# One rotation of three PSUM banks for the scores and the products with the values

## The chip, the cores and the metric

The kernel runs on one core of a Trainium2 chip. The metric is the device time of one launch in microseconds; lower is better. A time is the median of several runs on the chip; beside it stands one execution recorded by the hardware profiler, whose trace is read here.

## What is computed

Attention over four batches of eight heads (768 positions, head size 64), where a query sees the first four keys (the sinks) and the 128 keys up to its own position, followed by a feed-forward block with a short convolution as its gate. In the reference, cut to what matters:

```python
scores = scale * np.matmul(q, k.transpose(0, 1, 3, 2))
keep = is_sink | in_window            # 4 sinks, window of 128
scores = np.where(keep, scores, -1000000000.0)
a = np.exp(scores - np.max(scores, axis=-1, keepdims=True))
a = a / (np.sum(a, axis=-1, keepdims=True) + 1e-09)
x = np.matmul(a, v)                    # heads side by side: 512 columns
h = np.maximum(x @ w_in, 0.0)          # 512 -> 1024
conv_out = sum(conv_w[k] * shifted(h, k) for k in range(3))
out = (h / (1.0 + np.exp(-conv_out))) @ w_out
```

## The kernel before

The work goes by pairs of heads: 16 pairs g (four to a batch), each with six query tiles t of 128 rows. Three query tiles make a half. The first batch runs half 0 of its four pairs, then half 1 of each; from the second batch on, both halves of a pair follow each other. That gives 96 steps. Three slots of a step i work on three different steps:

- slot 0, `scores(g, t)` (L440): TensorE forms the scores of the two heads into two PSUM tiles `sc` (L319, or L322 and L323 from pair 4 on, where each product is split in two). VectorE patches the window edge (L457) and takes the row minimum of the negated, masked scores while writing them to SBUF as `pe` (L458). ScalarE takes the exponential (L461), VectorE the reciprocal of the sum (L463, L464), and GpSimd multiplies (L466).
- slot 1, `transp`, one step later: TensorE transposes `pe` into the PSUM tile `pts` (L481), ScalarE copies it to SBUF as `pT` (L483), GpSimd cuts the two triangles of the window (L485, L487). After the third tile of a half the sink columns are transposed too (L492 to L495, tile `tk`, result `sT`).
- slot 2, `pv`, two steps later and only after the third tile of a half: TensorE multiplies the values with `pT` (L512) and the sink part with `sT` (L515) into one PSUM tile `px` of 128x384. `xout` evacuates it with a ScalarE cast (L330, `xH`) and a VectorE subtraction (L331, `xL`), which together are the split operand of the feed-forward block.

The feed-forward block (`Moe`) works in units: 12 matmuls `ph` (L174), a chain over ScalarE, VectorE and GpSimd (L181 to L192), and six matmuls `po` (L201). It can start on a batch only when all four pairs of that batch have gone through `xout`. Its matmuls are handed out evenly between the slots while the next batch's attention runs, so TensorE has them to fill with; during the first 12 steps it has none. The feed-forward weights arrive in double width and are narrowed in those first steps (L102 to L105 and L112, L113, 16 tiles and the taps).

PSUM has eight banks here: two for `ph` and the transposes of q, k and sinks, two for `po`, one for `pts`, two for `sc` and one for `px`. A tile with a tag and `bufs=n` takes the next of n buffers in the order of the code, and waits until the last reader of that buffer's previous tile is through. A scheduler then orders the instructions of all engines by its own estimate of when each is ready, within these waits; the lists it makes are fixed when the kernel is built, and each engine works through its list in order. So on TensorE an instruction that waits holds up everything behind it in its list.

Of the kernel before, what the change touches and what calls it, by code (L numbers as in the profile page):

```python
# [10 lines left out]
F32 = mybir.dt.float32  # L11
# [6 lines left out]
P = 128  # L18
# [5 lines left out]
SW = 2 * P + NS  # L24
# [339 lines left out]
def banded(c):  # L364
# [8 lines left out]
    ap, ps = A.ap, A.ps  # L373
# [64 lines left out]
    def scores(g, t):  # L438
        s = st[g]
        lo = 0 if t == 0 else (t - 1) * KW  # L440
        mk = m0 if t == 0 else (m1 if t == 1 else m2)
        cols = slice(NS if t == 0 else 0, KW)
        sm = ap.tile([P, 6], F32, tag="sm", name=f"sm{g}_{t}", bufs=5)
        hf, u = divmod(t, 3)
        if u == 0:
            s.pe[hf] = ap.tile([P, 3, 2, KW], F32, tag="pe", name=f"pe{g}_{hf}")
            if t == 0:
                nc.gpsimd.memset(s.pe[hf][:, 0, :, 0:NS], 0.0)
        pe = s.pe[hf][:, u]
        pcs = [ps.tile([P, SW], F32, tag="sc", name=f"sc{g}_{t}_{j}", bufs=2) for j in range(2)]  # L450
        if t == 0:
            A.scores(s, t, [pc[:, KW:SW] for pc in pcs], lo, lo + P)
        else:
            A.scores(s, t, pcs, lo, lo + SW)
        for j, pc in enumerate(pcs):
            if t:
                nc.vector.copy_predicated(pc[:, KW:SW], before.bitcast(I32), pc[:, 0:P])  # L457
            nc.vector.tensor_tensor_reduce(out=pe[:, j, cols], in0=pc[:, P:SW][:, cols], in1=mk, op0=ALU.add, op1=ALU.min,  # L458
                                           scale=1.0, scalar=3.0e38, accum_out=sm[:, j:j + 1])
        for j in range(2):  # L460
            nc.scalar.activation(pe[:, j, cols], pe[:, j, cols], AF.Exp, bias=sm[:, j:j + 1], scale=-1.0,  # L461
                                 accum_out=sm[:, 2 + j:3 + j])
        nc.vector.tensor_scalar(sm[:, 2:4], sm[:, 2:4], 1e-9, None, ALU.add)  # L463
        nc.vector.reciprocal(sm[:, 4:6], sm[:, 2:4])  # L464
        for j in range(2):
            nc.gpsimd.tensor_scalar(pe[:, j, cols], pe[:, j, cols], sm[:, 4 + j:5 + j], 1.0, ALU.mult, ALU.mult)  # L466
# [30 lines left out]
    def pv(g, t):  # L497

        s = st[g]
        hp = g % NPAIR  # L500
        hf, u = divmod(t, 3)
        if u < 2:
            return
        px = ps.tile([P, 3, P], F32, tag="px", name=f"px{g}_{hf}").rearrange("p t k -> p (t k)")
        first = 3 * hf
        tiles = range(first + 2, max(0, first - 1) - 1, -1)
        for kt in tiles:
            pT = s.pT.pop((kt, hf)).rearrange("p h a k -> p h (a k)")
            lo, hi = max(kt, first), min(kt + 1, first + 2)
            cols = slice(P * (lo - kt), P * (hi - kt) + P)  # L510
            for j in range(2):
                nc.tensor.matmul(px[D * j:D * j + D, P * (lo - first):P * (hi - first) + P], s.v[:, kt, j, :], pT[:, j, cols],  # L512
                                 start=(kt == tiles[0]), stop=False, skip_group_check=True)
        for w in range(1 - hf, 3):
            nc.tensor.matmul(px[:, P * w:P * w + P], c.vs[:, w, P * hp:P * hp + P], s.sT, start=False, stop=(w == 2),  # L515
                             skip_group_check=True)
        A.xout(g, hf, px)
# [51 lines left out]
    for i in range(NST + D2):  # L569
        if i < NST:  # L570
            n, g, t = steps[i]
# [13 lines left out]
        for slot in range(SLOTS):  # L585
            if slot == 0 and i < NST:
                scores(g, t)
            if slot == 1 and 0 <= i - D1 < NST:
                transp(*steps[i - D1][1:])
            if slot == 2 and 0 <= i - D2 < NST:  # L590
                pv(*steps[i - D2][1:])
                if i - D2 + 1 in cuts:
                    while fill:
                        fill.pop(0)()
                    lo, hi, span = cuts[i - D2 + 1]
                    fill = m.pieces(lo, hi)
                    rate = len(fill) / (span - 0.5)
                    acc = 0.0
            acc += rate / SLOTS
            while acc >= 1.0 and fill:  # L600
                fill.pop(0)()
                acc -= 1.0
            while todo and i + (slot + 1) / SLOTS >= todo[0][0]:
                todo.pop(0)[1]()
# [143 lines left out]
```

## Time and profile before

| | |
|---|---|
| runs | 498.47, 500.34, 500.88 us, median 500.34 |
| the profiled execution | 500.05 us; its span in the trace 498.3 us |
| granted TensorE clock, mean of the span | 0.985 |
| HBM read and written | 27.65 MB and 6.29 MB |
| instructions on VectorE / ScalarE / GpSimd | 1176 / 1084 / 620 |

The span runs from the first to the last recorded instruction. "Busy" is the share of the span in which an engine ran something; PEld is TensorE's loading of stationary operands beside its matmuls. The waits view lists, for an engine and a line, which instruction of which engine ended its idle time, with the total in us, the number of waits and the longest. The timeline gives start, duration, engine, line, operation and tiles. The windows view gives busy time of each engine in a stretch, then the granted TensorE clock, the DMA share and GB/s. The product tiles `px` start at 27.29, 37.73, 45.28 and 49.83 us for half 0 of the first four pairs, at 61.72 for half 1 of pair 0, and the last one at 421.05 us.

### The profile page before, as it was taken

The page shows a single profiled execution, that of the slowest core. Times are in us where ns is not written, and L with a number is a line of the kernel's source. Part 1 is how long each engine was busy: PE and PEld are TensorE (multiplying, and loading weights), DVE is VectorE, ACT ScalarE, POOL GpSimd, SP SyncE. Part 2 cuts the span into 40 slices and gives each one's busy share as a digit, 9 for nine tenths or more (in the row PEclk, how much of TensorE's full clock was granted, in tenths as well). Part 3 has the DMA queues.
Part 4 walks back from the last instruction along what each step waited for, and adds up shares of the span by engine and source line. Part 5 has one row for each costly group of instructions (what it writes and reads, how often), then busy time and mean ns, then how long its engine had stood idle before and what let it go on. Part 6 is the DMA issues. An engine that isn't in the chain of part 4 may idle for free.

```text
span 498.3 us, 10547 instructions
## 1 busy us (share of the span) xinstructions
PE 464.8 (93%) x3209; PEld 398.1 (80%) x3209; DVE 351.4 (71%) x1176; ACT 341.7 (69%) x1084; POOL 322.6 (65%) x620
## 2 busy tenths in 40 slices
PE   3868879799999999999999999999999999999994
PEld 2546668588888888888888888888889888899982
DVE  5788989778857786867677777776585674655551
ACT  3979768678777967867777777776776664545542
POOL 2589899966866776685856677575755555344341
PEclk9999979999999999999999999999999999999999
DMA  5958652435234241514142333303011100101001
GB/s 124 261 154 216 204 135 66 101 80 141 60 70 100 74 112 35 140 34 97 37 100 53 70 90 72 99 18 95 24 54 34 42 3 2 42 1 43 8 36 51
DMA packets 85990, 39.59 MB, mean 79 GB/s; under 512 B 79244, under 2 KB 79268, under 8 KB 85924
## 3 DMA queue, kind: packets, MB, share of 16 engines
q1 hardware_dynamic: 85924, 38.82, 29.7%
q8 instruction: 28, 0.46, 0.4%
q14 instruction: 38, 0.31, 0.2%
HBM read 27.65 MB, written 6.29 MB: 68 GB/s over the span
## 4 chain that ended last, share of the span: by engine, by line
PE 81%; DVE 10%; POOL 3%; DMA 2%; ACT 2%; issue 2%; SPq 0%; DVEq 0%; ACTq 0%; POOLq 0%
PE ph L174 27%; PE po L201 26%; PE px L512 8%; PE sc L322 4%; PE pts L481 4%; PE px L515 4%; PE sc L323 3%; PE tq L261 2%; POOL pe L466 2%; PE sc L319 2%; PE tk L274 1%; DVE stm L104 1%; DVE stm L105 1%; DVE t L186 1%; DVE pe L458 1%
## 5 line engine op out<-in xcount | busy, mean ns | idle before, releaser
L201 PE MATMUL po<-woH,g 128*128 128x512 f32 x384 | 141.0, 408 | 5.5 <-POOL g L191 5.0
L466 POOL TENSOR_SCALAR pe<-pe,sm 128x132 f32<-128x132 f32 (+1 forms) x192 | 84.7, 452 | 49.8 <-DVE sm L464 30.7
L174 PE MATMUL ph<-xH,wiH 128*128 128x258 f32 (+1 forms) x384 | 112.2, 292 | 1.4 <-DVE kk L280 1.4
L174 PE MATMUL ph<-xH,wiL 128*128 128x258 f32 (+1 forms) x384 | 110.2, 287 | 0.0
L174 PE MATMUL ph<-xL,wiH 128*128 128x258 f32 (+1 forms) x384 | 110.0, 287 | 0.0
L461 ACT ACTIVATE pe<-pe,sm 128x132 f32<-128x132 f32 (+1 forms) x192 | 77.2, 405 | 21.1 <-DVE sm L458 20.5
L191 POOL TENSOR_SCALAR g<-t 128x256 fp32r<-128x256 f32 x96 | 41.7, 434 | 76.5 <-DVE t L189 55.0
L186 DVE SCALAR_TENSOR_TENSOR t<-hb,cw,t 128x256 f32<-128x256 f32 x96 | 60.4, 629 | 40.4 <-ACT t L185 39.6
L201 PEld LDWEIGHTS po<-woH,g 128*128 128x128 f32 x384 | 68.8, 189 | 16.1 <-POOL g L191 6.5
L174 PEld LDWEIGHTS ph<-xH,wiH 128*128 128x128 f32 x384 | 73.3, 191 | 4.6 <-issue 1.7
L201 PE MATMUL po<-woL,g 128*128 128x512 f32 x192 | 76.7, 399 | 0.0
L192 POOL TENSOR_TENSOR g<-t,g 128x256 fp32r<-128x256 f32 x96 | 73.0, 761 | 5.5
L174 PEld LDWEIGHTS ph<-xH,wiL 128*128 128x128 f32 x384 | 73.4, 191 | 2.3
L174 PEld LDWEIGHTS ph<-xL,wiH 128*128 128x128 f32 x384 | 73.2, 191 | 1.0
L188 ACT ACTIVATE t<-t 128x256 f32<-128x256 f32 x96 | 40.3, 419 | 36.3 <-DVE t L187 36.0
L457 DVE COPY_PREDICATED sc<-before,sc 128x128 f32<-128x128 int32 x160 | 44.7, 290 | 27.4 <-PE sc L323 19.0
L189 DVE SCALAR_TENSOR_TENSOR t<-t,hb 128x256 f32<-128x256 f32 x96 | 48.6, 507 | 19.4 <-ACT t L188 18.7
L458 DVE CUSTOM_DVE_ANT_0 pe<-sc,m 128x132 f32<-128x132 f32 (+1 forms) x192 | 52.5, 288 | 11.7 <-PE sc L323 9.0
L181 ACT ACTIVATE hb<-ph 128x258 f32<-128x258 f32 (+1 forms) x96 | 36.9, 386 | 29.6 <-PE ph L174 28.0
L187 DVE SCALAR_TENSOR_TENSOR t<-hb,cw,t 128x256 f32<-128x256 f32 x96 | 51.7, 538 | 4.7
L185 ACT ACTIVATE t<-hb,cw 128x256 f32<-128x256 f32 x96 | 49.2, 513 | 7.9 <-POOL g L192 4.0
L512 PE MATMUL px<-pT,vraw 128*64 128x256 f32 (+1 forms) x448 | 48.4, 345 | 3.0 <-POOL pT L487 3.0
(113 smaller groups left out, 943.5 us busy)
## 6 DMA issues: line engine op xcount, KB each, us to landing
raw<-in_q_dram SPq DMA_DIRECT2D x64, 96.0 KB
raw<-in_k_dram SPq DMA_DIRECT2D x64, 96.0 KB
out_dram<-stm SPq DMA_DIRECT2D x24, 256.0 KB
kk<-kk SPq DMA_DIRECT2D x24, 198.0 KB
vraw<-in_v_dram SPq DMA_DIRECT2D x24, 192.0 KB
wi_0r<-in_moe_w_in_dram SPq DMA_DIRECT2D x2, 512.0 KB
wi_1r<-in_moe_w_in_dram SPq DMA_DIRECT2D x2, 512.0 KB
wi_2r<-in_moe_w_in_dram SPq DMA_DIRECT2D x2, 512.0 KB
```

The costliest lines, as they stand in the source:

```text
L174: nc.tensor.matmul(u.h[:, 0:W], w[:, cc, ff * P:(ff + 1) * P], x[:, cc, t0:t1], start=(i == 0), stop=(i == len(prods) - 1))
L185: nc.scalar.mul(a, prev, cw[:, 0, ff:ff + 1])
L186: nc.vector.scalar_tensor_tensor(out=e, in0=this, scalar=cw[:, 1, ff:ff + 1], in1=a, op0=ALU.mult, op1=ALU.add)
L187: nc.vector.scalar_tensor_tensor(out=a, in0=nxt, scalar=cw[:, 2, ff:ff + 1], in1=e, op0=ALU.mult, op1=ALU.add)
L189: nc.vector.scalar_tensor_tensor(out=a, in0=e, scalar=1.0, in1=this, op0=ALU.add, op1=ALU.mult)
L192: nc.gpsimd.tensor_tensor(out=u.g[:, 1], in0=a, in1=f(u.g[:, 0]), op=ALU.subtract)
L201: nc.tensor.matmul(po[:, 0:c.DM], u.g[:, a, tt * P:(tt + 1) * P], w[:, ff, :], start=(ff == 0 and i == 0), stop=(ff == NFF - 1 and i == 2))
L457: nc.vector.copy_predicated(pc[:, KW:SW], before.bitcast(I32), pc[:, 0:P])
L458: nc.vector.tensor_tensor_reduce(out=pe[:, j, cols], in0=pc[:, P:SW][:, cols], in1=mk, op0=ALU.add, op1=ALU.min, scale=1.0, scalar=3.0e38, ...
L461: nc.scalar.activation(pe[:, j, cols], pe[:, j, cols], AF.Exp, bias=sm[:, j:j + 1], scale=-1.0, accum_out=sm[:, 2 + j:3 + j])
L466: nc.gpsimd.tensor_scalar(pe[:, j, cols], pe[:, j, cols], sm[:, 4 + j:5 + j], 1.0, ALU.mult, ALU.mult)
L512: nc.tensor.matmul(px[D * j:D * j + D, P * (lo - first):P * (hi - first) + P], s.v[:, kt, j, :], pT[:, j, cols], start=(kt == tiles[0]), s ...
```

## The change

The tile `px` takes the tag of the score tiles, and that tag gets three buffers in place of two. The number of banks in use stays at eight.

```diff
-        pcs = [ps.tile([P, SW], F32, tag="sc", name=f"sc{g}_{t}_{j}", bufs=2) for j in range(2)]
+        pcs = [ps.tile([P, SW], F32, tag="sc", name=f"sc{g}_{t}_{j}", bufs=3) for j in range(2)]
...
-        px = ps.tile([P, 3, P], F32, tag="px", name=f"px{g}_{hf}").rearrange("p t k -> p (t k)")
+        px = ps.tile([P, 3, P], F32, tag="sc", name=f"px{g}_{hf}", bufs=3).rearrange("p t k -> p (t k)")
```

Six score tiles and one `px` now follow each other through the same three banks, in the order of the code: `px` of a half comes behind the scores of the step two later than the half's last, and ahead of the next step's scores. Every engine's list changes with it, since the scheduler places instructions anew. Three places on TensorE follow. In the names, `sc1_2_0` is the score tile of pair 1, query tile 2, head 0; `px0_0` is the product tile of pair 0, half 0; `pe4_0` holds the weights of attention of pair 4, half 0; the last number of a name only tells instances apart.

The first is TensorE's list in the first stage, around the first product tile (difference of the two lists, - before, + changed):

```order
 L481 MATMUL pts_162<-ident_85,pe1_0_289 128x128 x2
-L319 MATMUL sc2_2_1_514<-kk2_277,X20_319 128x260
 L512 MATMUL px0_0_351<-pT0_2_0_305,vraw0_71 64x128 x2
 L512 MATMUL px0_0_351<-pT0_1_0_273,vraw0_71 64x256 x2
 L512 MATMUL px0_0_351<-pT0_0_0_234,vraw0_71 64x256 x2
 L515 MATMUL px0_0_351<-sT0_0_313,vs_156 128x128 x2
-L319 MATMUL sc3_0_0_546<-kk2_277,X30_447 128x128
+L319 MATMUL sc1_2_0_385<-kk0_163,X10_214 128x260
+L319 MATMUL sc1_2_1_386<-kk0_163,X10_214 128x260
```

Before, 18 score tiles stood ahead of `px0_0` (up to pair 2, tile 2); now 10 do, and the scores of pair 1, tile 2 come directly behind it.

The second is TensorE's list at the end of the product tile of pair 11, half 0. Before:

```order
L322 MATMUL sc12_0_1_4490<-kk4_1164,X120_4259 128x128
L323 MATMUL sc12_0_1_4490<-kk4_1164,X120_4259 128x128
L201 MATMUL po400_4233<-woH_111,g43_4277 128x512
L201 MATMUL po400_4233<-woL_112,g43_4277 128x512
L201 MATMUL po401_4237<-woH_111,g43_4277 128x512
L201 MATMUL po401_4237<-woL_112,g43_4277 128x512
L261 MATMUL tq1210_4376<-identr_90,nq121_4372 128x128 x3
L515 MATMUL px11_0_4397<-sT11_0_4323,vs_156 128x128 x2
```

And in the changed kernel:

```order
L174 MATMUL ph44_4325<-xL1_119,wiH_109 128x258
L481 MATMUL pts_162<-ident_85,pe11_1_4285 128x128
L261 MATMUL tq1210_4376<-identr_90,nq121_4372 128x128 x3
L481 MATMUL pts_162<-ident_85,pe11_1_4285 128x128
L515 MATMUL px11_0_4397<-sT11_0_4323,vs_156 128x128 x2
L322 MATMUL sc12_0_0_4489<-kk4_1164,X120_4259 128x128
L323 MATMUL sc12_0_0_4489<-kk4_1164,X120_4259 128x128
```

Between `px11_0` and `sc12_0_0` the code makes two score tiles (`sc11_5_0` and `sc11_5_1`), so `sc12_0_0` takes the bank of `px11_0`; it stood ahead of the last two matmuls of `px11_0` before and stands directly behind them now. The same neighbours stand at `px10_0` (two transposes between) and at `px14_0` (four matmuls of L201 between).

The third is TensorE's list between the scores of pair 4, tile 0 and their transposes. Before, the last rows ahead of the transposes (the scores `sc4_0_1` stand 28 rows ahead of these transposes, with 12 matmuls of L174 and 6 of L201 ahead of the first row shown):

```order
L481 MATMUL pts_162<-ident_85,pe3_1_1201 128x128 x2
L322 MATMUL sc4_1_0_1449<-kk4_1164,X40_1253 128x260
L323 MATMUL sc4_1_0_1449<-kk4_1164,X40_1253 128x260
L322 MATMUL sc4_1_1_1450<-kk4_1164,X40_1253 128x260
L323 MATMUL sc4_1_1_1450<-kk4_1164,X40_1253 128x260
L493 MATMUL tk3_5_1410<-ident_85,sk3_1_1411 96x128
L201 MATMUL po00_952<-woH_111,g6_1324 128x512
L201 MATMUL po01_992<-woH_111,g6_1324 128x512
L274 MATMUL tk50_1434<-ident_85,raw0_67 128x128 x3
L481 MATMUL pts_162<-ident_85,pe4_0_1384 128x128 x2
```

And in the changed kernel, from the scores themselves:

```order
L322 MATMUL sc4_0_1_1387<-kk4_1164,X40_1253 128x128
L323 MATMUL sc4_0_1_1387<-kk4_1164,X40_1253 128x128
L322 MATMUL sc4_1_0_1449<-kk4_1164,X40_1253 128x260
L323 MATMUL sc4_1_0_1449<-kk4_1164,X40_1253 128x260
L322 MATMUL sc4_1_1_1450<-kk4_1164,X40_1253 128x260
L323 MATMUL sc4_1_1_1450<-kk4_1164,X40_1253 128x260
L201 MATMUL po00_952<-woH_111,g6_1324 128x512
L201 MATMUL po01_992<-woH_111,g6_1324 128x512
L481 MATMUL pts_162<-ident_85,pe3_1_1201 128x128 x2
L493 MATMUL tk3_5_1410<-ident_85,sk3_1_1411 96x128
L274 MATMUL tk50_1434<-ident_85,raw0_67 128x128 x3
L481 MATMUL pts_162<-ident_85,pe4_0_1384 128x128 x2
```

The scores of tile 0 have moved towards their transposes: 12 matmuls of L174 and six of L201 no longer stand between them.

## The prediction, made before the changed kernel ran

> **What bounds the kernel now.** I read the page's totals first, then the stretches, then the waits of TensorE.
>
> ```profile
> span 498.3 us, 10547 instructions
> PE 464.8 (93%) x3209; PEld 398.1 (80%) x3209; DVE 351.4 (71%) x1176; ACT 341.7 (69%) x1084; POOL 322.6 (65%) x620
> PE 81%; DVE 10%; POOL 3%; DMA 2%; ACT 2%; issue 2%; SPq 0%; DVEq 0%; ACTq 0%; POOLq 0%
> ```
>
> TensorE is busy for 93% of the span and holds 81% of the chain that ended last. Where its missing 33.5 us lie, the stretches tell (busy us per engine, then granted clock, DMA share, GB/s):
>
> ```profile
> 10.00:20.00 10.00, 9.05 (x40) 6.79 (x41) 7.70 (x39) 8.47 (x28) 3.54 (x7) 1.00 0.88 208
> 20.00:30.00 10.00, 7.83 (x46) 5.04 (x45) 9.00 (x41) 9.59 (x38) 7.56 (x16) 1.00 0.74 214
> 30.00:40.00 10.00, 7.20 (x35) 4.70 (x36) 8.57 (x33) 7.24 (x27) 8.99 (x17) 0.83 0.61 190
> 40.00:50.00 10.00, 8.68 (x62) 6.42 (x62) 8.49 (x29) 9.23 (x29) 9.68 (x14) 1.00 0.82 212
> 50.00:60.00 10.00, 9.03 (x65) 7.67 (x64) 9.29 (x29) 7.53 (x27) 8.86 (x12) 1.00 0.62 194
> 60.00:70.00 10.00, 5.52 (x35) 3.83 (x34) 9.93 (x25) 6.92 (x19) 9.73 (x15) 0.82 0.63 171
> 70.00:80.00 10.00, 10.00 (x55) 8.91 (x54) 8.28 (x24) 6.84 (x20) 9.03 (x13) 0.84 0.27 74
> 110.00:430.00 320.00, 318.40 (x2338) 278.24 (x2338) 228.18 (x814) 233.72 (x768) 208.06 (x427) 1.00 0.26 67
> 430.00:498.30 68.30, 60.81 (x374) 53.91 (x373) 33.31 (x63) 29.00 (x67) 26.93 (x44) 0.99 0.07 25
> ```
>
> Two regimes. Up to about 80 us VectorE (third pair of numbers) and GpSimd are the fullest, since they narrow the feed-forward weights beside the first attention steps, and TensorE has gaps. From 110 to 430 us TensorE idles 1.6 us out of 320: there the other engines always deliver in time, and every wait that the change puts into TensorE's list is paid in full. After 430 us no attention is left, and the change touches nothing. So the question has two halves: what the first 80 us do, and whether the margins of the long middle hold.
>
> ```profile
> PE sc L319 <- DVE sm L458: 2.6, 6, 0.9
> PE sc L322 <- DVE sm L458: 0.9, 3, 0.4
> PE px L512 <- POOL pT L487: 3.0, 3, 1.4
> PE pts L481 <- POOL pe L466: 0.2, 1, 0.2
> ```
>
> These are TensorE's waits that the change bears on: 3.5 us for a free score bank, 3.0 us of the products for `pT`, and next to nothing of the transposes for the normalised weights.
>
> **Removed: waits for a score bank.** A third bank lets a score tile start a tile earlier, so at most the 3.5 us above go. Of them 2.6 are in the first stage (L319), where VectorE is the fuller engine and TensorE would only wait at the next place. Bounds 0 and -3.5; I take **-1.5**, nearer to the 0.9 of the middle than to the whole.
>
> **Added: a score tile behind the product tile in whose bank it goes.** The bank is free when L331 has ended. The quickest release in the middle, and a slow one:
>
> ```profile
> 202.57 0.94 PE L515 MATMUL px<-sT,vs 96*128 96x128 f32 x6
> 203.55 0.48 ACT L330 CAST xH<-px 128x384 fp32r<-128x384 f32 x1 [0.70 <-PE px L515]
> 204.06 0.56 DVE L331 TENSOR_TENSOR xL<-px,xH 128x384 fp32r<-128x384 f32 x1 [0.22 <-ACT xH L330]
> ...
> 156.96 0.83 PE L515 MATMUL px<-sT,vs 96*128 96x128 f32 x6
> 160.13 0.56 DVE L331 TENSOR_TENSOR xL<-px,xH 128x384 fp32r<-128x384 f32 x1
> ```
>
> From the end of the last L515 (203.51) to the end of L331 (204.62) are 1.11 us; in the slow case 160.69 - 157.79 = 2.9. In the new list `sc12_0_0` stands directly behind `px11_0`, and could start some 0.15 us before that matmul's modelled end: it waits 1.26 to 3.05 us. Behind `px10_0` stand two transposes (0.22 us), behind `px14_0` four L201 (0.94 us): 1.04 to 2.8, and 0.3 to 2.1. The other 21 such places of the middle have two us of work or more between. Sum 2.6 to 8 us, I take **+3.3**, near the quick row, since VectorE is busy for 71% only. Behind the waiting score stand all matmuls of the feed-forward block; nothing overtakes it.
>
> **Moved: scores nearer to their transposes.** One score tile's way to the normalised weights, in a common and in the shortest case:
>
> ```profile
> 200.25 0.37 PE L322 MATMUL sc<-kk,X 128*128 128x260 f32 x1
> 200.45 0.28 PE L323 MATMUL sc<-kk,X 128*128 128x260 f32 x1
> 200.57 0.63 PE L201 MATMUL po<-woH,g 128*128 128x512 f32 x2
> 201.91 0.27 DVE L458 CUSTOM_DVE_ANT_0 pe<-sc,m 128x132 f32<-128x132 f32 x1
> 203.67 0.17 DVE L464 RECIPROCAL sm<-sm 128x2 f32<-128x2 f32 x1
> 204.01 0.73 POOL L466 TENSOR_SCALAR pe<-pe,sm 128x132 f32<-128x132 f32 x2 [0.40 <-DVE sm L464]
> ...
> 391.81 0.28 PE L323 MATMUL sc<-kk,X 128*128 128x260 f32 x1
> 394.00 0.73 POOL L466 TENSOR_SCALAR pe<-pe,sm 128x132 f32<-128x132 f32 x2 [1.05 <-DVE sm L464]
> ```
>
> From the start of the second head's last score matmul to the end of L466: 204.74 - 200.45 = 4.29 us, and 394.73 - 391.81 = 2.92. TensorE must find that much other work in its list before the transposes. What it finds I add up from these rates:
>
> ```profile
> 118.84 1.47 PE ph L174 x12
> 412.61 2.81 PE po L201 x12
> 415.42 0.22 PE pts L481 x2
> 415.64 0.11 PE tk L493
> 200.00 0.49 PE L274 MATMUL tk<-ident,raw 128*128 128x128 f32 x3
> ```
>
> That is 0.12 us for one L174, 0.23 for one L201, 0.11 for one L481 or L493, 0.25 for three L274 (200.00 to 200.25) and 0.32 for a score tile (200.25 to 200.57). For pair 4, tile 0 the new list gives 0.12 (the rest of its own tile) + 2 x 0.32 + 2 x 0.23 + 2 x 0.11 + 0.11 + 0.25 = 1.8 us; the old one has 12 L174 and six L201 more between, 4.6 us. Such rates leave out the changes between kinds: between two products 180.9 us apart the same sum over the old list gives 168.8, 7% less.
>
> ```profile
> 226.48 1.52 PE L512 MATMUL px<-pT,vraw 128*64 128x128 f32 x16
> 407.39 1.30 PE L512 MATMUL px<-pT,vraw 128*64 128x128 f32 x12
> ```
>
> So I put 1.9 for 1.8. Done for all 72 steps of pairs 4 to 15, the new list has these below 4.29: 1.9, 2.8, 3.0, 3.0, 3.1, 3.3, 3.4, 3.5, 3.5, 3.6, 3.7, 4.1, 4.1; the old list 3.5 and 4.1. Most lie in pairs 4 to 9. Missing against 4.29: 12.8 us in sum, against 2.92: 1.1 us. The old list's two give 1.0 us by the first, while the trace has only the 0.2 us above in all; so the scheduler's close pairs are rather its quick ones, and a wait early in a chain lets the other engines catch up. I take **+4**, a third of the way from the lower bound.
>
> **Moved: the first stage.** Before `px0_0` now stand 10 score tiles, not 18, and each later product tile again waits for scores that stand behind the one before. Its spacing:
>
> ```profile
> 27.29 1.30 PE L512 MATMUL px<-pT,vraw 128*64 128x128 f32 x12 [0.77 <-POOL pT L487]
> 37.73 1.98 PE L512 MATMUL px<-pT,vraw 128*64 128x128 f32 x12
> 61.72 1.52 PE L512 MATMUL px<-pT,vraw 128*64 128x128 f32 x16 [1.44 <-POOL pT L487]
> 81.76 1.52 PE L512 MATMUL px<-pT,vraw 128*64 128x128 f32 x16
> ```
>
> The fifth product tile (pair 0, half 1) came at 61.72. If the first comes some 3 us sooner and each further one a lap of 10.4 us later (37.73 - 27.29), it comes at 24 + 42 = 66: 4 us late, 8 if the first gains nothing. Against that stands that VectorE has the same work either way: up to the eviction of pair 1, half 1 (at 81.76) its list holds 17 narrowed weight tiles and 5 gate chains before and after, and 42 score tiles before, 40 after; the weights now come between the laps, in place of scores. VectorE had 8.7 us idle from 10 to 80 us (70 less the sum of the third column); filling two thirds gains 6. Bounds -6 and +8, I take **+1**: near zero by the equal work, on the side of the laps. The weights' loads move up with their narrowing; DMA is busy for 0.61 to 0.88 here, so they can come a little sooner, not all at once.
>
> **Sum.** 500.05 (the profiled execution; its span is 498.3, the median of the runs 500.34) - 1.5 + 3.3 + 4 + 1 = 506.9: **507 us**, 1.3% slower than the median.
>
> **Rivals.**
> - *The margins hold* (no measurable change). The list's close pairs are the quick ones and meet the 2.92 us, the third bank gives its 3.5 us back: 500.05 - 3.5 + 2.6 + 1.1 = 500.3. For it: 1.6 us idle in 320 with the old list. Against: three scores directly behind their bank's products, which no speed of the chain excuses.
> - *The first stage gains* (faster). Narrowing weights between the laps fills VectorE's idle time: -6 - 1.5 + 3.3 = 496. For it: VectorE's equal work and 8.7 us idle. It decides if the fifth product tile starts before 61.7.
> - *The third bank pays in full* (faster): both rows of 3.5 us go from the end, and the scheduled distances cost nothing: 500.05 - 3.5 = 496.5. Against: 2.6 of them lie where VectorE is fuller than TensorE. The Trainium skill (Perfetto Trace Analysis, Matmuls) has the rule that speaks for it: independent matmul groups should rotate through different PSUM banks, so that the evacuation of one overlaps the next.
> - *The laps rule* (much slower): the fifth product tile some 8 us late, and chains of 4.29 us at two thirds of the close pairs: 500.05 + 8 + 3.3 + 8 = 519.
> - *The clock falls.* After 30 to 40 and 60 to 70 us, with 2.8 and 4.5 us of TensorE idle, the granted clock is 0.83, and 0.84 still in the full stretch from 70 to 80, which costs 1.6 us of ten. Three such dips in the middle put 5 us on top: 512. Against: the new waits are 1 to 2 us each. The Trainium skill (TensorE: Matmul & The Clock Gate, "A second HAM failure mode: psum-queue depth-cycling") tells of such a case: cycling through PSUM banks leaves small idle times that make the clock go up and down. The trace agrees only in part: from 10 to 70 us, with waits in every stretch, the clock stayed at 1.00 in four stretches of six.
>
> That the change does not do what it says is excluded by the lists: `sc1_2_0` follows `px0_0` now.
>
> **How the numbers follow.** Forecast 0.50, margins hold 0.20, first stage gains 0.09, third bank in full 0.04, laps rule 0.12, clock 0.05. The forecast's own range is 502 to 513. The range given, 498 to 516, leaves out most of the gain and the far end of the laps. A measurement of this kernel tells about 0.5% (2.5 us) from no change: faster 0.14, same 0.22, slower 0.64.
>
> **What would show it.** In the changed kernel the stretch from 110 to 430 us should hold 7 to 10 us of TensorE idle in place of 1.6; the waits should name a score behind L331 three times for 1 to 1.5 us, and transposes behind L466 about ten times for some 4 us; the first-stage waits of L319 for L458 should shrink; pair 1, half 1 should start its products at 79 to 86 us. The prediction is wrong if the middle stays at 2 us idle, or if that tile starts before 78 us.

## The result, and the profile after

| | before | changed |
|---|---|---|
| median of the runs, us | 499.73 (498.47 to 500.88) | 524.34 (523.98 to 524.84) |
| ratio, with its 95% interval | | 1.0494 [1.0464, 1.0523] |
| span of the profiled execution, us | 498.3 | 522.5 |
| start of the fifth `px` (pair 0, half 1), us | 61.72 | 85.20 |
| start of the last `px`, us | 421.05 | 444.15 |

The median before has one run more than the three above. The change makes the kernel 4.9% slower. Forecast was 507 us, within 498 to 516. The last product tile is 23.1 us late, of a span that is 24.2 us longer: the loss is made while attention runs, and what follows takes only 1.1 us longer than before.

Span, busy times and shares of the chain that ended last, from the changed kernel's page:

```profile
span 522.5 us, 10564 instructions
PE 474.2 (91%) x3209; PEld 400.2 (77%) x3209; DVE 347.7 (67%) x1176; ACT 343.4 (66%) x1084; POOL 322.2 (62%) x620
PE 70%; ACT 9%; DVE 9%; POOL 7%; issue 3%; DMA 2%; SPq 0%; DVEq 0%; POOLq 0%; ACTq 0%
```

No engine got fuller: VectorE and GpSimd have the work of before and a smaller share of a longer span. TensorE's part of the chain fell from 81% to 70%, and ScalarE, VectorE and GpSimd took it over: TensorE waits for them in turn. The stretches of the changed kernel (busy us of PE, PEld, DVE, ACT, POOL, then granted clock, DMA share, GB/s) show where:

```profile
20.00:30.00 10.00, 5.82 (x26) 3.64 (x25) 6.79 (x13) 6.67 (x21) 7.86 (x13) 0.72 0.78 226
30.00:40.00 10.00, 4.81 (x19) 2.60 (x17) 9.29 (x32) 6.65 (x23) 6.79 (x12) 0.84 0.65 217
40.00:50.00 10.00, 7.95 (x30) 5.06 (x30) 7.24 (x21) 6.19 (x16) 5.37 (x8) 0.67 0.48 150
50.00:60.00 10.00, 8.41 (x34) 4.95 (x33) 8.19 (x19) 6.12 (x16) 7.69 (x11) 0.57 0.67 185
60.00:70.00 10.00, 4.14 (x12) 2.18 (x13) 9.64 (x34) 6.55 (x20) 6.35 (x9) 0.77 0.38 120
110.00:430.00 320.00, 310.01 (x2259) 267.83 (x2259) 221.62 (x814) 229.24 (x769) 211.50 (x427) 0.99 0.28 69
```

From 20 to 70 us TensorE gets through 121 matmul records where it had 243 before (46 + 35 + 62 + 65 + 35). No engine is full in all of these stretches any more: from 40 to 50 us VectorE has 7.24, ScalarE 6.19 and GpSimd 5.37 us of ten, where VectorE had 8.49 and GpSimd 9.68. That is the mark of a serial chain rather than of a full engine. The middle idles 10.0 us on TensorE instead of 1.6.

The starts of the products, from the timeline of TensorE in the changed kernel (start, duration, what, and in brackets the wait before it):

```profile
25.63 2.40 PE L512 MATMUL px<-pT,vraw 128*64 128x128 f32 x12 [2.38 <-POOL pT L487]
40.82 2.40 PE L512 MATMUL px<-pT,vraw 128*64 128x128 f32 x12
55.34 2.40 PE L512 MATMUL px<-pT,vraw 128*64 128x128 f32 x12 [0.96 <-POOL pT L487]
76.54 1.30 PE L512 MATMUL px<-pT,vraw 128*64 128x128 f32 x12 [1.47 <-POOL pT L487]
85.20 1.52 PE L512 MATMUL px<-pT,vraw 128*64 128x128 f32 x16
```

The first comes 1.7 us sooner than before, and then the laps from one to the next are 15.2, 14.5, 21.2 and 8.7 us, where they were 10.4, 7.6, 4.6 and 11.9. The lap from 25.63 to 40.82 on TensorE:

```profile
27.96 1.22 PE L515 MATMUL px<-sT,vs 96*128 96x128 f32 x4
28.98 1.94 PE L319 MATMUL sc<-kk,X 128*128 128x260 f32 x4
...
31.45 1.62 PE L319 MATMUL sc<-kk,X 128*128 128x128 f32 x8
34.80 0.33 PE L481 MATMUL pts<-ident,pe 128*128 128x128 f32 x1 [1.74 <-POOL pe L466]
...
37.93 0.33 PE L481 MATMUL pts<-ident,pe 128*128 128x128 f32 x1 [2.00 <-POOL pe L466]
38.47 0.47 PE L481 MATMUL pts<-ident,pe 128*128 128x128 f32 x1 [0.21 <-POOL pe L448]
40.06 0.83 PE L481 MATMUL pts<-ident,pe 128*128 128x128 f32 x2 [1.11 <-POOL pe L466]
```

Six score tiles run in one burst behind `px0_0` (28.98 to 33.07), the first two of them the last of pair 1's half. Then TensorE has almost nothing but the transposes of what these scores become, one `pe` after the other, until `px1_0` can run. The scores of the next burst stand behind `px1_0` in the list.

### The profile page after: what moved, and what is told of

It is laid out like the page before. It is cut to its first block, busy times and chain, and to the rows that moved or that the text cites. A ratio compares the mean times of both kernels' runs of the same rounds, so it can differ in the third digit from the quotient of the medians.

```text
span 522.5 us, 10564 instructions
## 1 busy us (share of the span) xinstructions
PE 474.2 (91%) x3209; PEld 400.2 (77%) x3209; DVE 347.7 (67%) x1176; ACT 343.4 (66%) x1084; POOL 322.2 (62%) x620
## 4 chain that ended last, share of the span: by engine, by line
PE 70%; ACT 9%; DVE 9%; POOL 7%; issue 3%; DMA 2%; SPq 0%; DVEq 0%; POOLq 0%; ACTq 0%
PE ph L174 22%; PE po L201 22%; PE px L512 7%; PE px L515 4%; POOL pe L466 4%; PE pts L481 3%; ACT pe L461 3%; PE sc L322 3%; PE sc L323 2%; PE sc L319 2%; PE tq L261 1%; ACT X L240 1%; DVE stm L104 1%; PE tk L274 1%; POOL pT L485 1%
## 5 line engine op out<-in xcount | busy, mean ns | idle before, releaser
L201 PE MATMUL po<-woH,g 128*128 128x512 f32 x384 | 141.2, 411 | 3.0 <-POOL g L191 3.0
L466 POOL TENSOR_SCALAR pe<-pe,sm 128x132 f32<-128x132 f32 (+1 forms) x192 | 84.5, 452 | 48.2 <-DVE sm L464 23.5
L174 PE MATMUL ph<-xH,wiH 128*128 128x258 f32 (+1 forms) x384 | 112.0, 292 | 1.6 <-ACT sT L495 1.1
L174 PE MATMUL ph<-xL,wiH 128*128 128x258 f32 (+1 forms) x384 | 109.4, 285 | 0.0
L174 PE MATMUL ph<-xH,wiL 128*128 128x258 f32 (+1 forms) x384 | 109.2, 284 | 0.0
L186 DVE SCALAR_TENSOR_TENSOR t<-hb,cw,t 128x256 f32<-128x256 f32 x96 | 54.9, 572 | 53.8 <-ACT t L185 53.1
L201 PEld LDWEIGHTS po<-woH,g 128*128 128x128 f32 x384 | 68.7, 189 | 14.3 <-POOL g L191 5.1
L192 POOL TENSOR_TENSOR g<-t,g 128x256 fp32r<-128x256 f32 x96 | 74.5, 776 | 5.8
L174 PEld LDWEIGHTS ph<-xH,wiH 128*128 128x128 f32 x384 | 73.3, 191 | 5.0 <-ACT sT L495 1.5
L201 PE MATMUL po<-woL,g 128*128 128x512 f32 x192 | 76.4, 398 | 0.0
L174 PEld LDWEIGHTS ph<-xH,wiL 128*128 128x128 f32 x384 | 73.1, 190 | 1.9
L174 PEld LDWEIGHTS ph<-xL,wiH 128*128 128x128 f32 x384 | 72.9, 190 | 1.0
L189 DVE SCALAR_TENSOR_TENSOR t<-t,hb 128x256 f32<-128x256 f32 x96 | 46.7, 486 | 27.6 <-ACT t L188 26.8
L187 DVE SCALAR_TENSOR_TENSOR t<-hb,cw,t 128x256 f32<-128x256 f32 x96 | 52.9, 551 | 6.0
L458 DVE CUSTOM_DVE_ANT_0 pe<-sc,m 128x132 f32<-128x132 f32 (+1 forms) x192 | 52.3, 288 | 6.9 <-PE sc L323 4.0
L481 PE MATMUL pts<-ident,pe 128*128 128x128 f32 x192 | 44.0, 292 | 12.3 <-POOL pe L466 10.0
```

What stands on the lines that cost most here:

```text
L174: nc.tensor.matmul(u.h[:, 0:W], w[:, cc, ff * P:(ff + 1) * P], x[:, cc, t0:t1], start=(i == 0), stop=(i == len(prods) - 1))
L186: nc.vector.scalar_tensor_tensor(out=e, in0=this, scalar=cw[:, 1, ff:ff + 1], in1=a, op0=ALU.mult, op1=ALU.add)
L187: nc.vector.scalar_tensor_tensor(out=a, in0=nxt, scalar=cw[:, 2, ff:ff + 1], in1=e, op0=ALU.mult, op1=ALU.add)
L189: nc.vector.scalar_tensor_tensor(out=a, in0=e, scalar=1.0, in1=this, op0=ALU.add, op1=ALU.mult)
L192: nc.gpsimd.tensor_tensor(out=u.g[:, 1], in0=a, in1=f(u.g[:, 0]), op=ALU.subtract)
L201: nc.tensor.matmul(po[:, 0:c.DM], u.g[:, a, tt * P:(tt + 1) * P], w[:, ff, :], start=(ff == 0 and i == 0), stop=(ff == NFF - 1 and i == 2))
```

## The experiments

Two theories were set against each other at first. **Order theory**: one tag hands out its banks in the order of the code, so the scores behind a `px` can't pass it, and each lap is a chain from those scores to the next `px`. **Bank theory**: the shared banks themselves cost, since a score has to wait until the `px` in its bank is evacuated. Side theories were the narrowing of the weights, which the new lists put ahead of softmax steps, and the granted clock. Ratios are to the kernel before in the same series, with 95% intervals.

### Which part of the run

The shared rotation in the first batch alone, and from pair 4 on alone. The banks of `sc` and `px` are taken from a pool of their own, which is closed and opened anew after the first batch:

```diff
+A.sp = sco.enter_context(c.tc.tile_pool(name="scp0", bufs=1, space=PSUM))
...
+if slot == 0 and i == NSTB + D2:
+    sco.close(); A.nb = A.nl
+    A.sp = c.es.enter_context(c.tc.tile_pool(name="scp1", bufs=1, space=PSUM))
...
-pcs = [ps.tile([P, SW], F32, tag="sc", name=f"sc{g}_{t}_{j}", bufs=3) for j in range(2)]
+pcs = [A.sp.tile([P, SW], F32, tag="sc", name=f"sc{g}_{t}_{j}", bufs=A.nb) for j in range(2)]
...
+px = A.sp.tile([P, 3, P], F32, tag="sc" if A.nb == 3 else "px", name=f"px{g}_{hf}", bufs=3 if A.nb == 3 else 1)
```

`A.nb` is the number of score buffers: 3 and then 2 in the first kernel, 2 and then 3 in the second.

> One rotation of three banks for the first batch alone (pairs 0 to 3, 24 steps); after it a score pair of banks and a px bank of its own, as in the kernel before. First-stage theory: nearly the whole loss is made in the first 24 steps, so 517 to 522 us, pair 1 half 1 starts its products at about 100 us, and the middle idles 2 to 4 us on TensorE. Rival, middle theory (the loss is the sum of many waits in pairs 4 to 15): 502 to 507 us.

> The reverse: separate score and px banks in the first batch, one rotation of three from pair 4 on. First-stage theory: only the prediction's middle terms are left, 502 to 508 us, with pair 1 half 1 at about 82 us and 5 to 10 us of TensorE idle between 110 and 400 us. Rival, middle theory: 517 to 522 us.

Measured: first batch alone 520.77 us, 1.0429 [1.0403, 1.0455]; later batches alone 508.50 us, 1.0191 [1.0169, 1.0213]. The stretches from 20 to 100 and 110 to 430 us, first of the one with the first batch shared, then of the other:

```profile
20.00:100.00 80.00, 61.11 (x300) 43.10 (x300) 58.98 (x180) 52.71 (x159) 56.76 (x89) 0.79 0.46 132
110.00:430.00 320.00, 314.93 (x2285) 273.22 (x2285) 221.24 (x821) 231.62 (x773) 210.28 (x432) 0.99 0.27 69
```

```profile
20.00:100.00 80.00, 65.66 (x386) 49.65 (x385) 70.41 (x224) 60.96 (x195) 72.39 (x110) 0.91 0.57 156
110.00:430.00 320.00, 311.51 (x2270) 268.99 (x2267) 219.22 (x802) 226.93 (x753) 207.19 (x421) 0.99 0.26 65
```

The first batch makes most of it (22.3 us), and 300 matmul records from 20 to 100 us against 386 show it. Its middle idles 5.1 us, a little more than expected. The later batches make 10.0 us by themselves, half a us more than expected; TensorE's idle time in their middle is 8.5 us, against 1.6 before. Together that is more than the 24.6 us of the whole change, so the two parts do not simply add. What the change of pools costs by itself was not run.

### Order or banks

Three tags with one buffer each. In the first kernel scores and `px` take them in turn, so the three banks rotate as strictly as three banks can, but a tile waits for its own bank only. In the second, a control, scores take the first two and `px` the third, as before.

```diff
+def take(shared, product=False):
+    turn[shared] += not product or shared; return f"sc{2 if product and not shared else (turn[shared] - 1) % (2 + shared)}"
...
-px = ps.tile([P, 3, P], F32, tag="sc", name=f"px{g}_{hf}", bufs=3).rearrange("p t k -> p (t k)")
+px = ps.tile([P, 3, P], F32, tag=take(True, True), name=f"px{g}_{hf}", bufs=1).rearrange("p t k -> p (t k)")
```

> The same three banks in the same rotation for scores and px over the whole kernel, but as three tags with one buffer each, taken in turn, so that a tile waits only for the last tile of its own bank. The list then places 14, 17, 24, 30, 36, 42 score tiles ahead of the first six px tiles, where the changed kernel has 10, 16, 22, 28, 34, 40. Order theory (the loss comes from handing out one tag's buffers strictly in the order of the code, so that scores of the next steps can't pass a px): most of the first-stage loss goes, 498 to 508 us. Rival, bank theory (the loss comes from a score waiting until the px in its bank is evicted): 518 to 526 us, as in the changed kernel.

> Control for the way of writing: three tags with one buffer each, scores taking the first two in turn and px always the third, as the kernel before has its banks. All theories: 498 to 502 us, no change from the kernel before. If it is off by more than 3 us, the comparison of the three-tags kernel has to be made with this one.

Measured: three tags in turn 505.06 us, 1.0118 [1.0095, 1.0141]; tags apart 496.96 us, 0.9966 [0.9949, 0.9983]. Sharing with a freer order takes back 19 us of 25, with three banks for the same tiles. The control is 1.5 us faster than the kernel before in its series, a little under what all theories expected. From the three-tag kernel's waits of TensorE:

```profile
PE sc L319 <- DVE xL L331: 2.2, 1, 2.2
```

Here a score does sit in the bank of a `px` and waits 2.2 us for its evacuation, once. That is what the bank theory has in mind, and it is small. The three-tag kernel is still 8.1 us slower than its control; how much of that is due to the order and how much to the banks was not separated.

### The weights

> The changed kernel without the narrowing of 16 of the 17 weight tiles (L102 to L105 are left out; the high words of the weights are split as they stand), so that VectorE does 1.8 us and ScalarE 0.4 us less for each tile. To be read against the kernel before with the same left out. Weights theory (the first-stage loss comes from weight narrowing that the lists put ahead of the softmax steps): the gap between the two shrinks from 26 us to the middle's 4 to 9 us. Ring theory (each px waits for scores that wait for the px before, a lap of waits that would be there without the weights): a gap of 15 us or more is left.

> The kernel before with the same narrowing left out. Both theories: 485 to 499 us; it is the base for the changed kernel without narrowing.

```diff
-w = self.narrow(raw)
+w = raw if raw.dtype == F32 else f(raw[:, :, 1])
```

Measured: 510.85 us for the changed kernel, 484.65 us for the one before, 26.2 us apart, where 24.6 lie between the two with all the narrowing. From 20 to 100 us, first the changed kernel without narrowing, then the kernel before without it:

```profile
20.00:100.00 80.00, 66.47 (x361) 47.72 (x361) 38.37 (x158) 51.37 (x167) 55.15 (x102) 0.85 0.55 153
```

```profile
20.00:100.00 80.00, 71.41 (x487) 56.19 (x485) 57.28 (x216) 62.70 (x215) 67.03 (x125) 1.00 0.63 171
```

The starts of the first products, in the same order:

```profile
24.50 2.40 PE L512 MATMUL px<-pT,vraw 128*64 128x128 f32 x12
38.09 2.40 PE L512 MATMUL px<-pT,vraw 128*64 128x128 f32 x12 [1.50 <-POOL pT L487]
53.90 2.40 PE L512 MATMUL px<-pT,vraw 128*64 128x128 f32 x12 [1.14 <-POOL pT L487]
```

```profile
24.64 1.30 PE L512 MATMUL px<-pT,vraw 128*64 128x128 f32 x12
32.34 1.30 PE L512 MATMUL px<-pT,vraw 128*64 128x128 f32 x12
40.09 1.30 PE L512 MATMUL px<-pT,vraw 128*64 128x128 f32 x12
```

With VectorE busy for 38 us of 80 the laps are still 13.6 and 15.8 us, against 7.7 and 7.75. So the weights do not make the gap between the two kernels, and the weights theory falls. They are not free, though: without the narrowing the changed kernel is 13.5 us faster (524.34 - 510.85) and the one before 15.1 (499.73 - 484.65), so the narrowing costs both about the same.

### The clock

> The changed kernel without the narrowing of the weights, with two idle matmuls (128x512, their result read by nobody) after the scores of each of the steps 4 to 13, so that TensorE has less idle time in the laps; to be read against the same kernel without them (510.9 us). Clock theory (a good part of the loss is that the idle laps bring the granted clock down, 0.85 from 20 to 100 us against 1.00): the clock there rises over 0.95 and the time falls by 3 to 8 us. Ring theory alone (the laps are chains of waits, and the clock only follows): the time stays within 2 us or rises by up to 6, whatever the clock does.

```diff
 if slot == 0 and i < NST:
     scores(g, t)
+if slot == 0 and 4 <= i < 14:
+    wm = m.ps.tile([P, 512], F32, tag="po", name=f"warm{i}", bufs=NT)
+    for k in range(2):
+        nc.tensor.matmul(wm, c.ident[0:6 * SP], c.vs[:, 0], start=True, stop=True)
```

Measured: 512.64 us against 510.85 without the idle matmuls. In its timeline:

```profile
27.02 1.30 PE L512 MATMUL px<-pT,vraw 128*64 128x128 f32 x12
42.32 1.30 PE L512 MATMUL px<-pT,vraw 128*64 128x128 f32 x12
```

The twelve matmuls of a `px` take 1.30 us again instead of 2.40, at a granted clock of 1.00 up to 50 us, yet the lap is 15.3 us, after 13.6 without the idle matmuls. That does not clear the clock, though. The lap has six rows of idle matmuls (tile `warm`) like this one:

```profile
29.68 1.88 PE L591 MATMUL warm<-vs,ident 96*128 96x512 f32 x4
```

Together they hold TensorE for 11.3 us of the 15.3, and it idles nowhere in this lap. So they may have lengthened the lap by what the clock took off it, and the run does not tell the two apart. From 50 to 60 us, behind the last of them, the clock is 0.52, and over 20 to 100 us it comes to 0.91, short of the 0.95 expected.

What the low clock costs can be bounded from the stretches. From 20 to 100 us TensorE is busy for 58.86 us at a mean clock of 0.81 in the changed kernel, and for 64.77 us at 0.92 in the one before. If all of that time lay on the path and shrank in step with the clock, the low clock would cost 58.86 x 0.19 - 64.77 x 0.08 = 6 us more in the changed kernel. This is an estimate, and an upper one. The first stage loses about three times as much, so the clock may have a part in the loss but does not make most of it.

### The place of `px` in the order

The same shared tag of three buffers, with the products written elsewhere in the code. One step later:

```diff
-D1, D2 = 1, 2
+D1, D2 = 1, 3
```

> The changed kernel with the products written one step later in the code (three steps behind their scores instead of two), so px takes its place in the rotation two score tiles later: 12, 18, 24 ... score tiles ahead of it instead of 10, 16, 22. Order theory: the loss depends on how many scores stand ahead of px, so this takes back a third to a half of the first-stage loss: 511 to 519 us. Rival, bank theory (sharing the banks costs, wherever px stands): 521 to 527 us.

> The same with the products four steps behind their scores: 14, 20, 26 ... score tiles ahead of px. Order theory: about the number that the three-tags kernel had in the first stage, so 502 to 512 us. Rival, bank theory: 521 to 527 us.

Measured: 504.26 us, 1.0097 [1.0062, 1.0133], better than expected, and 505.99 us, 1.0131 [1.0101, 1.0161]. In both, the loads of the values come ahead of products that should still read the old ones. So the loads were moved along, behind the products of their step (and the loads of the sinks' values a step later, too):

```diff
-if n + 1 < len(jobs) and (t % 3 == 2 if n < 2 * NPAIR else t == 3):
-    values(n + 1)
...
+if slot == 2 and 0 <= i - 1 < NST:
+    n0, g0, t0 = steps[i - 1]
+    if n0 + 1 < len(jobs) and (t0 % 3 == 2 if n0 < 2 * NPAIR else t0 == 3):
+        values(n0 + 1)
```

> The kernel with the products one step later in the code again, now with the loads of the values moved one step later too: in the run without that, the products of some pairs read a later pair's values and may have waited for their load. Order theory: the same 502 to 508 us. If the wrong loads had helped: over 510 us.

> Control: the kernel before (px in a bank of its own) with its products and the loads of the values one step later in the code, too. Order theory: 497 to 502 us, no change, so that what the shared rotation gains from it is due to px's place in the rotation. If the later code order gains by itself (it moves the feed-forward units too): 490 to 496 us, and sharing would still cost 5 us or more.

Measured: shared and one step later 501.19 us, 1.0046 [1.0029, 1.0062]; the kernel before with the same move 501.45 us, 1.0057 [1.0040, 1.0074]. With `px` one step later, three shared banks cost nothing that can be measured against separate ones in the same code order. The shared one's products on the timeline, and its middle:

```profile
24.45 1.91 PE L512 MATMUL px<-pT,vraw 128*64 128x128 f32 x12 [0.72 <-POOL pT L487]
31.99 1.30 PE L512 MATMUL px<-pT,vraw 128*64 128x128 f32 x12 [0.20 <-DVE sm L464]
43.38 1.30 PE L512 MATMUL px<-pT,vraw 128*64 128x128 f32 x12 [2.27 <-POOL pT L487]
```

```profile
110.00:430.00 320.00, 319.87 (x2348) 279.03 (x2347) 226.41 (x813) 233.12 (x766) 211.67 (x430) 1.00 0.26 66
```

The first two laps are 7.5 and 11.4 us, and TensorE idles 0.1 us in the middle. Then the other way, one step earlier, with `pv` called ahead of `scores`:

```diff
+if slot == 0 and 0 <= i - D2 < NST:
+    pv(*steps[i - D2][1:])
 if slot == 0 and i < NST:
     scores(g, t)
...
 if slot == 2 and 0 <= i - D2 < NST:
-    pv(*steps[i - D2][1:])
```

> The changed kernel with the products written ahead of the scores of their step instead of behind them: the same three banks, but 8, 14, 20 ... score tiles ahead of px instead of 10, 16, 22. Now the last two score steps of the next half stand behind each px, and only the first ahead of it. Order theory (each lap from px to px is the chain of the scores that stand behind it): laps longer by another step's scores and weights of attention, 540 to 580 us. Bank theory (sharing costs, wherever px stands): 520 to 528 us.

Measured: 579.85 us, 1.1622 [1.1599, 1.1644]. Products and middle again:

```profile
23.45 2.40 PE L512 MATMUL px<-pT,vraw 128*64 128x128 f32 x12 [0.50 <-POOL pT L487]
42.39 2.40 PE L512 MATMUL px<-pT,vraw 128*64 128x128 f32 x12 [4.02 <-POOL pT L487]
```

```profile
110.00:430.00 320.00, 291.98 (x2001) 244.89 (x2002) 196.67 (x716) 208.48 (x685) 187.57 (x383) 0.96 0.27 68
```

Laps of 18.9 and, to the third `px` at 62.21, 19.8 us, and 28.0 us of idle time in the middle. By the place of `px`, the same three banks are 2 us, 25 us or 81 us slower than the kernel before. And one step later in the first batch only, with the loads moved as above:

```diff
-if slot == 2 and 0 <= i - D2 < NST:
-    pv(*steps[i - D2][1:])
+for k in [k for k in (i - 3, i - 2) if slot == 2 and 0 <= k < NST and (i - k == 3) == (k < NSTB)]:
+    pv(*steps[k][1:])
```

> Products one step later in the code for the first batch alone (12, 18, 24 ... 54 score tiles ahead), from pair 4 on as in the changed kernel (58, 64, 70). Order theory, with the loss of the later batches kept and that of the first stage gone: as the kernel with separate banks in the first batch, 504 to 511 us. If px's place matters in the later batches as little as the rival says: 499 to 503 us, as the kernel with px later everywhere.

Measured: 505.43 us, 1.0134 [1.0117, 1.0151]. The first stage's part is thus 18 to 19 us (18.9 by 524.34 - 505.43, from two series; 18.0 by their ratios), that of the later batches some 7.

Two steps later is one too many:

> The changed kernel with the products and the loads of the values two steps later in the code: 14, 20, 26 score tiles ahead of px. Order theory: the scores are free enough with one step already, so 498 to 505 us; the feed-forward block starts a step later, which may cost 1 to 3 us. Bank theory: 520 to 528 us.

```diff
-s.sT = ap.tile([6 * SP, P], F32, tag="sT", name=f"sT{g}_{hf}")
+s.pT["s", hf] = ap.tile([6 * SP, P], F32, tag="sT", name=f"sT{g}_{hf}")
```

> Products two steps later once more (14, 20, 26 score tiles ahead of px), now with a sink tile sT kept for each half: in the two runs before, the products of half 0 of pairs 4 to 15 read the sink weights of half 1, and had to wait for that half's transposes. Order theory: 498 to 505 us, no more gain than with one step. If the later code order costs by itself, whatever px waits for: 508 to 512 us again.

Measured: 510.75 us, where half 0 of pairs 4 to 15 read the other half's sink weights, and 509.60 us, 1.0203 [1.0178, 1.0228], where each read its own. Both missed what was expected. The last `px` group of the latter starts at 428.23 us of a span of 508.4, so some 80 us follow, 3 more than before, and the rest lies ahead of it. Why the second step costs was not settled: the kernel before with the products two steps later was not run, so the second step may cost without any sharing, too.

### Two more that missed

```diff
-px = ps.tile([P, 3, P], F32, tag="sc", name=f"px{g}_{hf}", bufs=3)
+px = (m.ps if g < NPAIR and not hf else ps).tile([P, 3, P], F32, tag="po" if g < NPAIR and not hf else "sc",
+     name=f"px{g}_{hf}", bufs=2 if g < NPAIR and not hf else 3)
```

> The changed kernel, but the first four px tiles (half 0 of pairs 0 to 3) take a buffer of the po tag, which the feed-forward block does not use yet; from the fifth px on all is as in the changed kernel. The list has 12, 14, 24, 30 score tiles ahead of these four, then 34, 40, 46 as in the changed kernel. Ring theory (each lap of the rotation costs where no feed-forward work stands beside it, that is in the first four laps above all): 505 to 515 us. Rival (the laps from the fifth px on cost as much each): 517 to 523 us.

Measured: 526.26 us, 1.0553 [1.0514, 1.0592]: no gain. The fourth `px` starts at 63.30 instead of 76.54 us, but the next lap is 16.8 us, and by the last one all is lost again. In the `po` tag these `px` stand in line with the transposes of q and k, so the run does not tell the laps apart; the kernel with the products one step later in the first batch alone does that.

```diff
-u.h = self.ps.tile([P, 512], F32, tag="h", name=f"ph{n}", bufs=2)
+u.h = self.ps.tile([P, 512], F32, tag=self.turn(), name=f"ph{n}", bufs=1)
```

> The control with three tags of one buffer each, with the two h buffers (feed-forward products, transposes of q, k and sinks) written as two tags of one buffer as well, taken in turn, so that a tile waits only for its own buffer there too. Order theory (handing out one tag's buffers in the order of the code costs also where two tiles share it): 490 to 497 us, faster than the kernel before by up to 2%. Rival (the order only costs where a px stands between scores): 496 to 501 us.

Measured: 507.91 us, 1.0167 [1.0146, 1.0187], above what either theory expected. More freedom for the order is not a gain by itself.

### A version that beats both

> The control with three tags of one buffer each (scores in the first two, px in the third) once more, since it came out at 0.9966 of the kernel before. If that gain is real: 0.994 to 0.999, 495 to 498 us, and it beats both kernels by a little. If it was chance: an interval that takes in 1.000.

Measured: 496.13 us, 0.9938 [0.9922, 0.9953]. Banks as before, written as three tags of one buffer, are faster than the kernel before by 0.3 and 0.6% in two series. TensorE's matmuls come in the same order up to the scores of pair 7, tile 0, and in another behind them; what in it brings the gain was not tried.

| score tiles ahead of the first four `px` | code | us |
|---|---|---|
| 8, 14, 20, 26 | shared, one step earlier | 579.85 |
| 10, 16, 22, 28 | shared, the change | 524.34 |
| 12, 18, 24, 30 | shared, one step later | 501.19 |
| 14, 20, 26, 32 | shared, two steps later | 509.60 |
| 14, 17, 24, 30 | three tags in turn | 505.06 |
| 18, 24, 27, 30 | the kernel before | 499.73 |

The medians come from several series, in which the kernel before stands at 498.47 to 499.75 us.

## Why the prediction was right in direction and wrong in size

**First stage, +1 us: the step that failed.** It was about +18 to +22 (18 to 19 by the kernel with `px` later in the first batch, 22 by the one that shares in the first batch alone). The mechanism was named, the laps, but the term was mis-sized twice. First, the lap was put at 10.4 us, from the old spacing of `px0_0` and `px1_0`, and the fifth `px` at 66 us. The four laps measured 14.9 us on average (59.6 in sum, from 25.63), and the fifth `px` started at 85.20. In the old list the scores of the next half run ahead of `px0_0`, so that spacing is an overlapped one. In the new list a half's last scores stand behind the `px` before, and the lap is that `px` and then the whole way from the scores to their own `px`: 3.4 us from 25.63 to the scores at 28.98, and 11.8 us from there to `px1_0` at 40.82. The old trace gave a warning. By the list, the last score tile of pair 1's half is this row of the kernel before:

```profile
20.81 0.68 PE L319 MATMUL sc<-kk,X 128*128 128x260 f32 x2
```

From 20.81 to `px1_0` at 37.73 are 16.9 us. That is an upper figure, since `px1_0` may have waited for other things as well, and as a size it is too long; but it shows that the way can be longer than the 10.4 us taken. Second, equal work on VectorE was taken for a reason to bring the term down to +1. Work that is equal does not keep an engine filled when the chain through it is serial: VectorE was busy for 58.86 us from 20 to 100 us, and for 70.35 before.

**Removed waits, -1.5: none went.** From the changed kernel's waits of TensorE:

```profile
PE sc L319 <- DVE sm L458: 4.0, 4, 1.4
PE sc L319 <- DVE xL L331: 2.4, 2, 1.5
```

With 0.2 us at L322, scores wait 4.2 us for L458, after 3.5 (2.6 + 0.9).

**A score behind the `px` in its bank, +3.3: void.** The prediction, like the section on the change, took it that tiles always follow each other through the banks in turn, so that `sc12_0_0` gets the bank of `px11_0`. It does not. The changed kernel's timeline at this place, over all engines:

```profile
322.06 0.61 PE L515 MATMUL px<-sT,vs 96*128 96x128 f32 x4
322.43 0.31 PE L322 MATMUL sc<-kk,X 128*128 128x128 f32 x1
...
323.87 0.48 ACT L330 CAST xH<-px 128x384 fp32r<-128x384 f32 x1
324.54 0.54 DVE L331 TENSOR_TENSOR xL<-px,xH 128x384 fp32r<-128x384 f32 x1
```

`sc12_0_0` runs at 322.43, before `px11_0` is evacuated: the two readers of `px11_0` start at 323.87 and 324.54. So it can't be in its bank. No wait for L331 stands in the middle at all; the two there are (2.4 us, above) lie in the first stage, and they are what the bank theory has for itself in this kernel.

**Scores nearer to their transposes, +4: right in part, and half the size measured.** The waits of TensorE from 110 to 430 us in the changed kernel:

```profile
PE pts L481 <- POOL pe L466: 2.4, 4, 1.0
PE po L201 <- POOL g L191: 1.8, 4, 0.8
PE tk L493 <- ACT sk L492: 1.7, 2, 1.5
PE pts L481 <- ACT pT L483: 1.3, 2, 0.7
PE ph L174 <- ACT sT L495: 1.1, 1, 1.1
PE px L512 <- POOL pT L487: 0.9, 2, 0.7
```

These 9.2 us are met at several links of the way from scores to products and on to the feed-forward block; only 2.4 of them are the wait that the prediction named, transposes behind L466. The middle idles 8.4 us more than before; the two terms had 7.3 together, so their sum came out right by luck, from an error in each. That the order makes this part too shows in the kernel with `px` one step later, where the middle idles 0.1 us.

Three smaller slips in the prediction change little: +4 lies a quarter of the way between its bounds of 1.1 and 12.8, not a third; the fifth `px` comes 7 us late, not 8, if the first gains nothing (27.3 + 41.6 against 61.7); and from 10 to 30 us ScalarE is fuller than VectorE (8.47 and 9.59 us of ten against 7.70 and 9.00).

**The rivals.** The first stage did not gain (the fifth `px` was to start before 61.7), and the margins did not hold. The laps rule was the nearest, at 519 us, though with a lap that was still too short. The third bank did not pay: with the same code order, one step later, three shared banks and two and one apart come to 501.19 and 501.45 us. The rule of the Trainium skill (Perfetto Trace Analysis, Matmuls), that independent matmul groups should rotate through different PSUM banks, is kept in both of these, and the third bank in the rotation brought nothing by itself. The clock did fall, but in the first stage, to 0.57 from 50 to 60 us, not in the middle (0.99); by the estimate above it made at most some 6 us there. Of the signs that were named, the middle's idle time (7 to 10 us) came true. The others did not: pair 1, half 1 started at 100.59 us and not at 79 to 86, no score in the middle waits behind L331, the first-stage waits of L319 for L458 grew, and the transposes wait 10.0 us for L466 in twelve waits, of which 7.6 us lie in the first stage, and not some 4.

## What to carry to other kernels

When two kinds of tile share one tag, look first at the order in which the code asks for them: what is asked for after a tile that comes late is stuck behind it. Size such a ring by the late tile itself and the way from the tiles behind it to the next late one, bounded from the trace, and not by the spacing in an old list that overlaps. If the banks have to be shared, ask for the late tile later in the code, one step here, and measure, since a step more cost again; tags of one buffer each, which let later tiles pass, brought back most of the loss, too.

## What the runs showed of the hardware

In the changed kernel the granted clock was 0.57 to 0.84 in the stretches from 20 to 70 us, where TensorE idled 1.6 to 5.9 us of every ten, and the same twelve matmuls took 2.40 us instead of 1.30. The idle time of a stretch does not tell the clock, though. With `px` one step later TensorE idled 4.0 us from 40 to 50 us, and the clock was 1.00 there and 0.96 in the ten us after; with the idle matmuls it idled 3.8 us in the same stretch, at a clock of 1.00, and had 0.52 in the ten us after. The idle matmuls held the clock at 1.00 from 20 to 50 us, but took 11.3 us of a lap for themselves, and the time did not gain (512.64 after 510.85 us).
